# Attention and a leaky-ReLU layer pair on one core: the first two batches by thirds of 192 tokens

## The chip, the core and the metric

The kernel runs on one core of a Trainium2 chip. The metric is device time in microseconds (us) of the whole kernel, the median of several runs. A profile of one execution gives the span (first to last instruction) and what every engine did in it: PE (matmuls; PEld are its weight loads), DVE, ACT and POOL (elementwise work), SP (it issues most DMAs), and the 16 DMA engines.

## The reference

Eight batches, eight heads, 576 tokens, head size 64. Heads 0 to 3 ("plain") see the last 32 tokens; heads 4 to 7 ("dilated") see the last 32 tokens at distance 0, 4, 8, ... The heads' outputs side by side are the rows `x` (4608 x 512) of two weight matrices with a leaky ReLU between them.

```python
mask_plain = (rel >= 0) & (rel < window)                       # window = 32
mask_dil = (rel >= 0) & (rel < window * dilation) & (rel % dilation == 0)   # dilation = 4
scores = np.where(mask, scale * q @ k.T, -1e9)
attn = softmax(scores)
x = (attn @ v), heads side by side
h = x @ w_in                       # 512 -> 2048
out = np.maximum(0.01 * h, h) @ w_out   # 2048 -> 512
```

## The kernel before

**Tiling.** Tokens are taken in fours: token 4n + r is row n, residue r, so that a dilated head of one residue is a plain window over n. Two batches make a pair m; a pair's 1152 rows are three chunks of 384 columns in `xt`: chunk 0 is the first 384 of batch 0, chunk 1 the first 384 of batch 1, chunk 2 the last 192 of both. For every chunk there are 16 "ups" (`up`, four matmuls over the 512 inputs, then a leaky ReLU by ACT into `gt`) and three "downs" of 128 rows (`down`, 16 matmuls, an eviction, stores). From the ninth tile on, four tiles go together through `group`, with fewer products and sums of weights; the last three chunks take `up_fast`.

**Attention of the first two batches** (`b < EARLY`). `load_group` loads q, k and v of one kind of heads: 128 rows of four tokens, that is 512 of the 576 tokens, as 128 partitions x 1 KB per head. POOL, DVE or ACT cast them to fp16 (L272, L270) into `nat`. `turn` lets PE transpose four 128 x 128 blocks each of q and k (L692) and moves them from PSUM into `slots` (L644, L642) in the order that the scores need. `unit` is one set of scores, exponential, mask, values and norm: in `BY_PE` the mask is added by a matmul with the identity (L837), the scores are L854 (or L840), the values L898 (or L892) and the sums L886; ACT forms the reciprocal as exp(-ln), and DVE multiplies into `xt` (L936). A dilated unit covers two residues x 96 rows, or, for the last 48 rows, four residues x 48 ("small"). The last 64 tokens come apart (`load_rest`, `part == 1`): loads of 16 rows per head into `stg[4]` and into every fourth partition of v, a cast into `rest`, 8 transposes for all heads. For batch 0 the plain heads' v is not loaded a second time in its overlapping layout; PE makes it from the rows with shifted identities (`permute`, L347, and L353 for the rest). Later batches are loaded in another layout (128-byte packets to 32 partitions) and turned by DVE and POOL (L674, L679, L685), in `late_unit` and `across`.

**Weights.** `load_w` brings w_in in 8 blocks of 512 KB (n = 0 to 7: row block n % 4, column half n // 4) and w_out in 8; POOL and DVE cast them in halves. An up of columns j needs the four row blocks of its column half.

**Order.** The whole program is a list of tasks with dependencies, a cost and a priority each. `_Plan.run` places them on engines by these costs, and the program issues them in that order. On the chip every engine works its own list in order and waits on semaphores. `FIRST` writes out the order of SP's first loads: b and v are q, k and v of batch 0 by kind of heads, i and o are blocks of w_in and w_out, 0 is the rest of batch 0, c, y and 1 the same of batch 1. `RANKS` gives the priorities of the attention parts. Buffers are rings (`ring`): a new user waits for the last user of its slot. Where the plan leaves PE a gap, filler matmuls on the tile `warm` into a spare bank are put in (L1595); eight stand at the start (L1489).

```python
FIRST = "bvbviiii0iiiicoocoyoooooy1"
...
first_ups = [up(0, j, 0, 384, x_done[0, 0], first_acts) for j in range(N_UPS)]
...
halves = [(0, 192), (192, 192)] if m == 0 and n_c % 3 == 2 else [(0, 384)]
```

Chunk 0's ups start when batch 0's first part has been normed; the other eight of its ups come later in the plan, by the due times `begins` (20.8 us a chunk). PSUM has eight banks: `sps0`, `tp`, two `ops`, two `hps` (ups), two `fps` (downs). During batch 0's first part `fps[1]` also takes k's transposes, and `hps` scores and values.

Of the kernel before, what the change touches and what calls it, by code (L numbers as in the profile page):

```python
# [14 lines left out]
WIN = 32  # L15
AHEAD, LATE = 5.0, 4.0
# [4 lines left out]
FIRST = "bvbviiii0iiiicoocoyoooooy1"  # L21
RANKS = ((10.0, 6.0), (10.0, 0.5), (15.0, 2.0), (25.0, 2.0))


def _constants():

    ident = np.eye(128, dtype=np.float16)
    p = np.arange(128)[:, None]
    key = p - 32
    c = np.arange(96)[None, :]  # L30
    qry = 4 * (c % 24) + c // 24
    rel = qry - key
    band = (rel >= 0) & (rel < WIN)
    first = band & (key >= 0)
    rel0 = c - p
    d0 = (rel0 >= 0) & (rel0 < WIN)
    c1 = np.arange(48)[None, :]
    rel1 = 96 + c1 - (16 + p)
    d1 = (rel1 >= 0) & (rel1 < WIN)
    rel2 = 96 + c1 - np.where((p < 64) & (p % 4 == 0), 128 + p // 4, p)  # L40
    d2 = (rel2 >= 0) & (rel2 < WIN)
    bias = np.where(np.concatenate([first, band, band, d0, d2], axis=1), 0.0, -60000.0)
    parts = [ident, bias, first, band, band, d0, d1, d1, d0, d2]
    return np.concatenate([x.astype(np.float16) for x in parts], axis=1)
# [98 lines left out]
def kernel(  # L143
# [24 lines left out]
    TILED = ((0, 0), (0, 1), (1, 0))  # L168
    BY_PE = ((0, 0), (0, 1), (1, 0))
    POOL_MASK = (1,)  # L170
    BLOCKS = tuple(range(16))
    N_UPS = 8
# [20 lines left out]
    NBIAS, NMASK = 288 + 96 + 48, 288 + 288 + 48  # L193
# [3 lines left out]
    B_PL, B_D0, B_D2 = 128, 128 + 288, 128 + 288 + 96  # L197
# [8 lines left out]
    vst = [v_all[:, 2048 * i:2048 * i + 2048] for i in range(2)]  # L206
    v_two = [v_all[:, 1024 * i:1024 * i + 1024] for i in range(NVS)]
# [37 lines left out]
    tpk = fps[1].bitcast(FP16)  # L245
# [6 lines left out]
    def took(n, size):  # L252
        for a, ta, b, tb in ((4, 9.0, 128, 15.0), (128, 15.0, 256, 19.0), (256, 19.0, 1024, 48.0),
                             (1024, 48.0, 2048, 85.0)):
            if size <= b:
                return n * (ta + (tb - ta) * (size - a) / (b - a)) / 16e3
        return n * size / 25.6 / 16e3

    def load(queue, dst, src, n, size, deps, prio, slow=1.0):
# [3 lines left out]
                        LATE if prio > -1500 + len(FIRST) else 0.8 if prio >= AFTER else 0.0)  # L263
# [35 lines left out]
    def clear_slots(slots, prio, deps):  # L299
        for i in slots:  # L300
            t_zero[i] = ([clear("DVE", qbd[i][64:128, 0:S], 0.34, 0.0, prio, deps),
                          clear("DVE", qbd[i][0:64, S:2 * S], 0.34, 0.0, prio, deps)],
                         [clear("DVE", kt[i][:, 0:PAD], 0.1, 0.0, prio, deps)])

    clear_slots(range(4), -2000, [])
    t_one = clear("POOL", ones, 0.1, 1.0, -1995)
    t_ones = {}
    TWO_ONES = float(np.ones(2, np.float16).view(np.float32)[0])

    def clear_ones(slots, deps, prio=-700):  # L310
        for i in slots:
            t_ones["d", i] = clear("POOL", at(vd[i].bitcast(FP32), 0, 128, D // 2, [64, 16], [1, D // 2]),
                                   0.48, TWO_ONES, prio,
                                   deps)
            t_ones["p", i] = clear("POOL", at(vp[i].bitcast(FP32), 0, 128, D // 2, [64, 12], [1, D // 2]),
                                   0.38, TWO_ONES, prio,
                                   deps)

    clear_ones(range(2), [], -1980)
    t_vr = [clear("POOL", vst[i][0:64, 1024:2048], 1.0, 0.0, -1970 + i) for i in range(2)]  # L320
    SPREAD, SHIFT = 36, 67

    def ident_at(tl, off, step, prio):
        t = clear("DVE", tl.bitcast(FP32), 0.3, 0.0, prio)
        return add("DVE", 0.2, 0.2, [t, t_id], lambda e: nc.vector.tensor_copy(
            out=at(tl, 0, 128, off, [step, 128]), in_=ident), prio)

    t_spread = ident_at(el[0], SPREAD, 4, -1985)
    t_shift = ident_at(el[1], SHIFT, 1, -1600)
    v_half = pair1  # L330
    permuted = []

    def permute(tiles, deps, prio, rest_from=None):

        if rest_from is None:
            n, b_users = tiles[0] // 2, []
            b_old = rings["TPK"][-1] if n else []
            bk = fps[n]
        else:
            n, b_old = ring("F", 2, b_users := [])  # L340
            bk = fps[n]

        def pe(e):
            for y, t in enumerate(tiles):
                for r in range(4):
                    s = 96 * t - 32 - r + SPREAD
# [3 lines left out]
                if t == 5:  # L350
                    for r in range(4):
                        for i in range(2):
                            nc.tensor.matmul(bk[:, 256 * y + 128 * i:256 * y + 128 * i + 128],  # L353
                                             el[1][0:64, 3 - r:131 - r],
                                             at(turned[i], 0, 64, r * D, [256, 2], [1, D]),
                                             start=False, stop=(r == 3), skip_group_check=True)
        t_p = add("PE", 0.11 * (4 * len(tiles) + 4 * (5 in tiles)), 0.25,
                  deps + b_old + [t_spread] + [t_shift] * (5 in tiles), pe, prio)
        permuted.append((t_p, b_users))
        res = []  # L360
        for j in range(2):
            vt = vp[j]

            def fn(e, j=j, vt=vt):
                o = at(vt, 0, 128, tiles[0] * 128, [768, 2], [128, 2], [1, D])
# [5 lines left out]
            t = add((("ACT", 0.3), ("DVE", 0.36)), None, 0.2, [t_p] + kept_old[j], fn, prio)  # L371
            b_users.append(t)
            res.append(t)
        if rest_from is None:
            rings["F"][n].extend(res)
# [4 lines left out]

    kept, v_late, seen_ones = {}, {}, {}
    kept_old = [[], []]

    def stage_slot(early, users):
        if early:
            return ring("STG", NST, users)
        if "STG4" not in rings:
            assert len(rings["STG"]) == 2 * NST
            rings["STG4"] = rings["STG"][-NST:-1]
        return ring("STG4", NST - 1, users)  # L390
# [5 lines left out]
    def load_group(b, g, prio, prio_v):  # L396
# [3 lines left out]
        early = b < EARLY  # L400
        first = b == 0
        base = (b * H + 4 * g) * HS
        stage, loads = [], []
        for o, src in ((0, q), (1, k)):
            sn, s_old = stage_slot(early, s_users := [])
            st = stg[sn]
            if first:
                lo = [load("SP", at(st, 0, 128, j * 512, [256, 2], [1, 256]),
                           dram(src, base + 2 * j * HS, [4 * D, 128], [HS, 2], [1, 256]),
                           256, 1024, s_old, prio + 0.3 * j + 0.1 * o) for j in range(2)]  # L410
            elif early:
                lo = [load("SP", at(st, 0, 128, 0, [256, 4], [1, 256]),
                           dram(src, base, [4 * D, 128], [HS, 4], [1, 256]),
                           512, 1024, s_old, prio)]
            else:
                lo = [load("SP", at(st, 32 * a, 32 * a + 32, 0, [32, 36], [1, 32]),
                           dram(src, base + (a // 2) * 2 * HS + (a % 2) * 32,
                                [D, 32], [32 * D, 36], [1, 32]),
                           1152, 128, s_old, prio) for a in range(4)]
# [3 lines left out]
        lv, v_free = [], []  # L423
        if early:
            vn, v_old = ring("VST", 2, v_users := [])
            vs = vst[vn]
            v_free = [v_users, v_users]
            if dil:
                lv = [[load("SP", at(vs, 0, 128, 0, [256, 4], [1, 256]),
                            dram(v, base, [4 * D, 128], [HS, 4], [1, 256]), 512, 1024, v_old,  # L430
                            prio_v)]] * 2
                v_late[b] = vs, v_old, v_users
            if first and not dil:
                t_l = load("SP", at(vs, 0, 128, 0, [256, 4], [1, 256]),
                           dram(v, base, [4 * D, 128], [HS, 4], [1, 256]), 512, 1024, v_old, prio_v)
                c_h = [cast(v_half[:, 512 * i:512 * i + 512], vs[:, 512 * i:512 * i + 512], 512, [t_l],
                            prio_v, ("POOL", "ACT")) for i in range(2)]
                v_users += c_h
                v_late[b, 0] = vs, v_old, v_users
                v_late["cast"] = c_h  # L440
                made = [{0: [], 1: []}, {0: [], 1: []}]
            for j in range(2 if not dil and not first else 0):
                n = 12
                lj = [load("SP", at(vs, 0, 128, (12 * j + 12 - n) * D, [D, n], [1, D]),
                           dram(v, base + (1152 * j - 32) * D, [D, 128], [96 * D, n],
                                [1, D]), 128 * n, 256, v_old, prio_v + 0.3 * j)]
                lv.append(lj)
            v_from = [(vs, 2 * j * (256 if dil else 384), 256 if dil else 384) for j in range(2)]
        else:
            if "V2" not in rings:  # L450
                rings["V2"] = [sum(rings["VST"][-2:], [])] * NVS
# [206 lines left out]
    def turn(b, hp, part, prio):  # L658
# [89 lines left out]
        else:  # L748
# [39 lines left out]
            if b:  # L788
                ev += q_users
# [863 lines left out]
```

## Time and profile before

| what | value |
|---|---|
| median of 3 runs | 305.9 us (305.5 to 306.68) |
| the profiled execution | 306.29 us |
| its span | 304.5 us |
| PE busy | 294.4 us (97%), 2970 matmuls |
| DVE, ACT, POOL busy | 231.0, 188.7, 132.3 us |
| DMA | 51.09 MB, mean 168 GB/s |
| granted TensorE clock | 1.0 |
| last store done after the last matmul's end | 3.8 us |

The profile also lists the costliest groups of instructions (columns: line, engine, operation, output<-inputs, shapes, count | busy us, mean ns of one | idle before):

```profile
L1091 PE MATMUL hps<-xt,w_in 128*128 128x384 f16 (+1 forms) x640 | 111.7, 310 | 0.8 <-DVE w_in L272 0.6
L1364 PE MATMUL fps<-w_out,gt 128*128 128x256 f16 x416 | 53.6, 273 | 0.0
L272 POOL CAST nat<-stg 128x576 f16<-128x576 f32 (+1 forms) x53 | 43.0, 834 | 9.7 <-DMA stg<-in_q_dram 3.5
```

Matmuls overlap, so the mean of one is longer than the distance from one start to the next; what a matmul takes of PE's time is that distance. The filler counts as busy too.

### The profile page before, as it was taken

Reading aid. Unit: us, or ns where it says so; the run is one execution under the profiler, and the core shown is the slowest. Engines: PE = TensorE matmul, PEld = TensorE weight load, DVE = VectorE, ACT = ScalarE, POOL = GpSimd, SP = SyncE. Lnnn points to the kernel's source line nnn. Section 1 sums busy time; section 2 is a strip of 40 time slices with the busy share of each in tenths; the row PEclk is TensorE's granted clock in tenths of the full one; section 3 lists DMA queues with packets and bytes.
Section 4 is the critical chain, followed back from the end, with each engine's and each line's share of the span. In section 5 each row is a group of like instructions: output and inputs, shape, how many; then the busy total and the mean of one; then the engine's idle time right before and its main releaser. Section 6 shows DMA issues by size and latency. Waiting matters only on the chain.

```text
span 304.5 us, 7869 instructions
## 1 busy us (share of the span) xinstructions
PE 294.4 (97%) x2970; PEld 225.4 (74%) x2970; DVE 231.0 (76%) x478; ACT 188.7 (62%) x458; POOL 132.3 (43%) x179
## 2 busy tenths in 40 slices
PE   6889999999999999997999999999999999999994
PEld 3646655667777676786777777887788999999984
DVE  6875875689686869959888779879775899697552
ACT  3857854795556678464766567456565688767230
POOL 5469555393674949159094668665000000000000
PEclk9999999999999999999999999999999999999999
DMA  7999999999999899976999969793102110031124
GB/s 241 404 370 392 407 289 201 239 201 167 253 171 196 190 188 196 174 180 134 183 161 221 204 136 194 159 208 80 37 2 72 34 37 2 11 91 32 32 76 146
DMA packets 160390, 51.09 MB, mean 168 GB/s; under 512 B 137632, under 2 KB 157024, under 8 KB 160352
## 3 DMA queue, kind: packets, MB, share of 16 engines
q1 hardware_dynamic: 159520, 49.86, 68.3%
q10 hardware_dynamic: 832, 0.73, 0.8%
q8 instruction: 23, 0.38, 0.5%
q14 instruction: 15, 0.12, 0.1%
HBM read 41.13 MB, written 9.44 MB: 166 GB/s over the span
## 4 chain that ended last, share of the span: by engine, by line
PE 90%; DVE 5%; ACT 3%; DMA 1%; issue 1%; DVEq 0%
PE hps L1091 29%; PE fps L1364 26%; PE fps L1275 9%; PE ops L1015 3%; PE hps L1188 3%; PE ops L1188 3%; PE ops L1063 2%; PE sps L1188 2%; PE tp L1188 1%; PE tp L692 1%; PE ops L1364 1%; PE tp L982 1%; PE sps L982 1%; DVE ee L1008 1%; PE fps L347 1%; PE tp L975 1%
## 5 line engine op out<-in xcount | busy, mean ns | idle before, releaser
L1091 PE MATMUL hps<-xt,w_in 128*128 128x384 f16 (+1 forms) x640 | 111.7, 310 | 0.8 <-DVE w_in L272 0.6
L1102 ACT ACTIVATE gt<-hps 128x384 f16<-128x384 f32 (+1 forms) x160 | 72.8, 461 | 43.8 <-PE hps L1091 41.5
L1091 PEld LDWEIGHTS <-w_in 128*128 128x128 f16 x640 | 56.7, 98 | 26.3 <-DVE w_in L272 1.0
L1364 PEld LDWEIGHTS <-gt 128*128 128x128 f16 x672 | 64.4, 98 | 9.7
L679 POOL COPY slots<-turned 64x576 f16<-64x576 f16 x48 | 36.3, 757 | 47.4 <-DVE turned L674 45.5
L1364 PE MATMUL fps<-w_out,gt 128*128 128x256 f16 x416 | 53.6, 273 | 0.0
L272 POOL CAST nat<-stg 128x576 f16<-128x576 f32 (+1 forms) x53 | 43.0, 834 | 9.7 <-DMA stg<-in_q_dram 3.5
L1275 PE MATMUL fps<-w_out,gt 128*128 128x512 f16 x128 | 32.4, 379 | 0.0
L1037 DVE TENSOR_TENSOR rc<-ops,recs 96x384 f16<-96x384 f32 x48 | 25.7, 538 | 0.3
L1393 ACT COPY stg<-fps 128x512 f32<-128x512 f32 (+1 forms) x24 | 12.8, 532 | 14.4 <-PE fps L1364 14.4
L1008 DVE TENSOR_TENSOR ee<-ee,con 128x576 f16<-128x576 f16 x24 | 17.2, 722 | 3.5 <-ACT ee L994 3.5
L1033 DVE RECIPROCAL recs<-ops 96x6 f32<-96x6 f32 x48 | 8.7, 181 | 14.7 <-PE ops L1015 12.5
L1401 DVE TENSOR_TENSOR osb<-fps,stg 128x512 f32<-128x512 f32 x18 | 12.4, 687 | 9.7 <-PE fps L1364 5.6
L272 POOL CAST vd<-v_all 128x1024 f16<-128x1024 f32 (+2 forms) x20 | 18.0, 918 | 2.7 <-DMA v_all<-in_v_dram 2.7
L1211 ACT ACTIVATE gt<-stg 128x384 f16<-128x384 f32 x36 | 18.0, 524 | 1.1 <-DVE stg L1205 1.1
L1275 PEld LDWEIGHTS <-gt 128*128 128x128 f16 x128 | 11.6, 98 | 9.1
L644 DVE COPY slots<-tp 64x128 f16<-64x128 f16 (+7 forms) x42 | 13.4, 333 | 6.3 <-PE tp L692 5.6
L674 DVE STREAM_TRANSPOSE turned<-nat 128x576 f16<-128x576 f16 x24 | 17.7, 751 | 0.0
L685 DVE STREAM_TRANSPOSE slots<-nat 128x576 f16<-128x576 f16 x24 | 17.7, 745 | 0.0
L1008 DVE TENSOR_TENSOR el<-el,con 128x576 f16<-128x576 f16 x24 | 15.0, 630 | 2.7 <-ACT el L994 2.5
L1188 PEld LDWEIGHTS <-w_in 128*128 128x128 f16 x192 | 16.4, 98 | 0.5 <-DVE w_in L1119 0.3
L994 ACT ACTIVATE ee<-sps 128x288 f16<-128x288 f32 x24 | 9.8, 409 | 8.4 <-PE sps L982 5.8
(158 smaller groups left out, 529.3 us busy)
## 6 DMA issues: line engine op xcount, KB each, us to landing
stg<-in_q_dram SPq DMA_DIRECT2D x48, 144.0 KB, 3.2
stg<-in_k_dram SPq DMA_DIRECT2D x48, 144.0 KB, 2.9
v_all<-in_v_dram SPq DMA_DIRECT2D x24, 256.0 KB, 3.8
v_all<-in_v_dram SPq DMA_DIRECT2D x24, 192.0 KB, 3.2
gt<-in_moe_w_in_dram SPq DMA_DIRECT2D x5, 512.0 KB, 7.1
out_dram<-osb SPq DMA_DIRECT2D x22, 96.0 KB, 2.0
out_dram<-osb SPq DMA_DIRECT2D x40, 48.0 KB, 1.8
out_dram<-osb SPq DMA_DIRECT2D x25, 64.0 KB, 2.2
```

The lines of the kernel that those rows point to most:

```text
L272: ENG[e].tensor_copy(out=dst, in_=src)
L674: lambda e: nc.vector.transpose(xb, na[:, 0:S]), prio)
L679: lambda e, p0=p0, hh=hh: nc.gpsimd.tensor_copy(out=at(qb, p0, p0 + 64, hh * S + o, *od), in_=at(xb, p0, p0 + 64, i, *id_)), prio, 0.0, "m ...
L685: lambda e: nc.vector.transpose(kb[:, PAD:PAD + S], na[:, S:2 * S]), prio)
L1008: nc.vector.tensor_tensor(out=x, in0=x, in1=mk, op=ALU.mult)
L1037: nc.vector.tensor_tensor(out=at(xb, 0, 96, 768 * n + 64 * i, [256, 3], [128, 2], [1, D]), in0=at(ot, 0, 96, 0, [130, 3], [65, 2], [1, D]) ...
L1091: nc.tensor.matmul(ht[:, 0:n], at(w_in, 0, 128, i * DFF + j // 2 * 256 + j % 2, [2, 128]), at(xt[m % 2], 0, 128, i * 1152 + x0, *dims), st ...
L1102: lambda e: nc.scalar.activation(out=gt[c % NG][:, j * n_c + x:j * n_c + x + n], in_=ht[:, 0:n], func=AF.Prelu, alpha=0.01),
L1188: nc.tensor.matmul(cell[:, n * z:n * z + n], lhs(2 * p + z, i), rhs(i), start=first and z == 0 and i == 0, stop=z == 1 and i == 1, skip_gr ...
L1211: lambda e: nc.scalar.activation(out=at(g, 0, 128, j * n_c + n * y, [n_c, 2], [1, n]), in_=at(src, 0, 128, 0, [n, 2], [1, n]), func=AF.Pre ...
L1275: nc.tensor.matmul(ft, g[:, j * n_c + tt * 128:j * n_c + tt * 128 + 128], w_out[:, j * DM:j * DM + DM], start=(j == 0), stop=(j == NJ - 1))
L1364: nc.tensor.matmul(bk[:, x:x + HN], tl[:, off + j * step:off + j * step + 128], rhs(j), start=first and x == 0 and j == 0, stop=j == HJ - ...
```

## The change

The first two batches are no longer taken as 512 tokens and a rest of 64 but as three thirds of 192 tokens (48 rows of four). `load_third` loads, for each kind of heads, q to partitions 0 to 47 and k to 48 to 95 of one tile, with four heads x 1 KB per partition, and v to 48 partitions (64 to 111 or 16 to 63 in turn). One cast takes q and k of two heads together on 96 partitions, one set of transposes turns both (96 x 128 blocks, `turn_third`), and each move serves two heads. All dilated units are now of the small form (48 rows x 4 residues), with k of the current and the last third side by side in `kt`. `permute` makes v of batch 0 by third; in batch 1 the plain v is loaded in its layout, two loads a third.

Chunk 0's ups are cut in two halves of 192 columns (the first third, the second third) by `up_half`: pairs of j share a bank and one leaky ReLU. Chunk 2's ups stay in halves; the first of them depends on batch 0 alone and is now placed with batch 0 (`UPS`). Masks by PE are now in five of the six thirds (`BY_PE`), twenty units as before. `FIRST` and `RANKS` are written anew (A, a to F, f are the thirds and their v), as are some constants of the planner (`LATE`, `took`). `load_rest`, the shifted identity in `el[1]`, and `part` are gone.

```diff
-AHEAD, LATE = 5.0, 4.0
+AHEAD, LATE = 5.0, 2.5
-FIRST = "bvbviiii0iiiicoocoyoooooy1"
-RANKS = ((10.0, 6.0), (10.0, 0.5), (15.0, 2.0), (25.0, 2.0))
+FIRST = "AaiiBbiiiiiiCcooooDdooooEeFf"
+RANKS = ((-30.0, 5.0), (-8.0, 0.1), (-6.0, 0.1), (-4.0, 0.1), (-3.0, 0.1), (20.0, 2.0))
...
-    TILED = ((0, 0), (0, 1), (1, 0))
-    BY_PE = ((0, 0), (0, 1), (1, 0))
+    BY_PE = ((0, 0), (0, 1), (0, 2), (1, 0), (1, 1))
...
+    def load_third(b, t, prio, prio_v):
+        for g in (1, 0):
+            dil = g == 1
+            base = (b * H + 4 * g) * HS + 192 * t * D
+            sn, s_old = ring("STG", NST - 1, s_users := [])
+            st = stg[sn]
+            lo = [load("SP", at(st, 48 * o, 48 * o + 48, 0, [256, 4], [1, 256]),
+                       dram(src, base, [4 * D, 48], [HS, 4], [1, 256]),
+                       192, 1024, s_old, prio + 0.4 * (1 - g) + 0.1 * o)
+                  for o, src in ((0, q), (1, k))]
...
+            c_qk = [cast(at(na, 0, 96, 512 * j, [D, 2], [128, 4], [1, D]),
+                         at(st, 0, 96, 512 * j, [256, 2], [D, 4], [1, D]), 512, lo + n_old,
+                         prio + 0.4 * (1 - g), ("DVE", "ACT", "POOL") if b == 0 else CENG) for j in range(2)]
...
+        even = t % 2 == 0
+        d0, p0 = (64, 16) if even else (16, 64)
+        ld = load("SP", at(vs, d0, d0 + 48, 0, [256, 4], [1, 256]),
+                  dram(v, base, [4 * D, 48], [HS, 4], [1, 256]), 192, 1024, v_old, prio_v)
...
+    def turn_third(b, t, g, prio):
+            def pe(e, j=j):
+                for r in range(4):
+                    nc.tensor.transpose(bk[:, 384 * j + 96 * r:384 * j + 96 * r + 96],
+                                        na[0:96, 512 * j + 128 * r:512 * j + 128 * r + 128],
+                                        ident[0:96, 0:96])
...
+    def up_half(c, y, p, done, acc):
+        x0, x_in, x_out = ((48 * y, [[96, 4], [1, 48]], [[48, 4], [1, 48]]) if c == 0 else
+                           (384 + S * y, [[1, 192]], [[1, 192]]))
+        def part_of(i):
+            def fn(e):
+                for z in range(2):
+                    nc.tensor.matmul(ht[:, 192 * z:192 * z + 192],
+                                     at(w_in, 0, 128, i * DFF + p * 256 + z, [2, 128]),
+                                     at(xt[0], 0, 128, i * 1152 + x0, *x_in),
...
+    UP_AT = {0: (0.0, 5.2), 2: (12.0, 45.0)}
+    UPS = (((0, 0, 0),), ((0, 0, 4), (0, 1, 0), (0, 1, 4)), ((2, 0, 0), (2, 0, 4)))
...
+                    if b == 0:
+                        for c, y, p in [(c, y, p) for c, y, p0 in UPS[t] for p in range(p0, p0 + 4)]:
+                            acts = all_acts.setdefault(c, [[] for _ in range(NJ)])
+                            up_half(c, y, p, x_done[c, y], acts)
```

## The prediction

> **What bounds the kernel now.** I first read busy time by stretches of 5 us (columns: the stretch, then the busy time of PE, its weight loads, DVE, ACT and POOL with instructions, the granted clock, the DMA share, GB/s).
>
> ```profile
> 0.00:5.00 5.00, 3.71 (x10) 1.28 (x10) 3.42 (x17) 1.33 (x2) 3.85 (x12) 1.00 0.56 180
> 15.00:20.00 5.00, 4.71 (x47) 2.53 (x44) 4.48 (x12) 3.37 (x11) 2.50 (x5) 1.00 1.05 356
> 20.00:25.00 5.00, 4.16 (x30) 2.35 (x29) 2.98 (x11) 2.34 (x5) 5.00 (x9) 1.00 1.03 386
> 25.00:30.00 5.00, 5.00 (x53) 3.36 (x52) 2.92 (x7) 3.64 (x9) 5.00 (x12) 1.00 1.06 403
> 35.00:40.00 5.00, 5.00 (x43) 3.19 (x41) 3.25 (x9) 2.78 (x7) 2.99 (x6) 1.00 1.03 420
> ```
>
> From 25 us PE has no idle time and its clock is full; until 40 us the DMA share is 1.0 too. So PE is busy to the end once it has work, and what can be won is the time before. PE's timeline shows where that begins (start, duration, instruction, idle before):
>
> ```profile
> 18.00 1.25 PE L1595 MATMUL fps<-warm 128*128 128x512 f16 x5
> 19.09 1.16 PE L1091 MATMUL hps<-xt,w_in 128*128 128x384 f16 x6
> 20.89 0.50 PE L1091 MATMUL hps<-xt,w_in 128*128 128x384 f16 x2 [0.64 <-DVE w_in L272]
> 21.22 0.38 PE L1595 MATMUL fps<-warm 128*128 128x512 f16 x1
> 21.80 1.46 PE L1091 MATMUL hps<-xt,w_in 128*128 128x384 f16 x8 [0.20 <-ACT gt L1102]
> ...
> 103.04 0.68 PE L1063 MATMUL ops<-con,rc 96*128 96x96 f16 x12
> ...
> 142.55 0.36 PE L1015 MATMUL ops<-vp,ee 128*128 128x65 f16 x6 [1.60 <-DVE ee L1008]
> ```
>
> L1595 on "warm" is filler, useful to nobody; the last is at 21.22. From 21.80 to the last matmul PE waits only twice, 0.17 us at 121.8 and 1.60 us at 142.5; then 3.8 us of eviction and store. Work done by 21.8, priced by distance between starts: 8 times 4 transposes at 0.23 = 1.84; 8 units with scores at 0.33 and values at 0.30 = 5.04; 16 spreading matmuls (L347) at 0.11 = 1.76; 8 up-projections at 0.1625 = 1.30. Sum 9.9, so **11.9 us are lost** at the start.
>
> What keeps PE waiting is data. POOL's timeline shows the weight blocks landing, and the one-microsecond stretches the rates:
>
> ```profile
> 13.48 0.61 POOL L272 CAST w_in<-gt 128x512 f16<-128x512 f32 x1 [0.65 <-DMA gt<-in_moe_w_in_dram]
> 14.76 0.61 POOL L272 CAST w_in<-gt 128x512 f16<-128x512 f32 x1 [0.66 <-DMA gt<-in_moe_w_in_dram]
> 16.04 0.61 POOL L272 CAST w_in<-wst 128x512 f16<-128x512 f32 x1 [0.67 <-DMA wst<-in_moe_w_in_dram]
> ...
> 8.00:9.00 1.00, 0.61 (x7) 0.21 (x4) 0.64 (x2) 0.98 (x3) 0.93 (x2) 1.00 1.07 377
> 13.00:14.00 1.00, 0.76 (x8) 0.50 (x6) 0.97 (x3) 1.00 (x3) 0.52 (x1) 1.00 1.05 430
> 17.00:18.00 1.00, 0.71 (x8) 0.29 (x6) 0.73 (x3) 1.00 (x5) 0.12 (x1) 1.00 1.12 290
> ...
> 46.00:50.00 4.00, 4.00 (x34) 2.19 (x33) 2.06 (x6) 1.92 (x6) 2.90 (x5) 1.00 1.21 192
> ```
>
> Blocks of 512 KB come every 1.28 us (about 415 GB/s); q, k and v, in packets of 1 KB, move at about 376 (377 at 8 us). The dip at 17 us is where the small loads of the last 64 tokens run (`load_rest`), which the change drops. Block 0's cast starts 0.9 us after its last byte by the summed rates; I use 0.9 as landing delay.
>
> **The change, part by part.**
>
> *PE work.* Transposes: 80 at 57.5 ns (0.23/4) become 96 over 96 partitions; row 103.04 is that form, 12 in 0.51 us to the next start, 42.5 ns: 4.60 to 4.08, -0.52. Spreading: 1.76 at 13.46 us plus 0.97 and 0.55 at 26.48 (3.28) becomes 24 at 0.11 (2.64): -0.64. Eight dilated units have 8 value matmuls of 48 columns (0.14) for 4 of 96 (0.11): +0.24. Chunk 0's up-projection is 128 of 192 columns (0.0825, from 0.66 for 8) for 64 of 384 (0.1625): +0.16. Scores cost the same (4 x 0.041 against 2 x 0.0825), masks by PE stay 20, chunk 2 was in halves already. Sum **-0.76 us**, all of it on PE's path.
>
> *When data arrives.* SP's new order is third A of batch 0 (q and k of the dilated heads, then of the plain ones, then two v loads; six loads, 1.18 MB), two w_in blocks, third B, six w_in, C, w_out blocks, D and so on. SP issues a load in 0.51 us, 0.197 MB each, 386 GB/s, so issue doesn't bound. By before's summed bytes for the first 6 us, then 376 and 415: A complete at 6.25 (with constants), two blocks 8.8, B 11.9, six blocks 19.5, C's first pair 20.55. With 0.9 landing: B's second q,k pair 11.7, w_in block 3 15.3, block 7 20.4, C's first pair 21.4, D's 30.1, E's 39.65. DVE's clears end near 5.0, as before (4.92): two of `kt` grow from 0.1 to about the 0.30 of a 64x288 one, one clear of `el` and one copy (0.5 together) go. POOL clears three v tiles (0.92 each), five 512-word tiles (0.47) and two of 384 (0.40), 6.0 us with `ones` against 3.7, so it is free at 6.7; its first cast waits for v at 7.0 anyway. 0 on the path; if v came at once, 0.5.
>
> *PE's walk*, in its own order:
> 1. The second group of B is transposed after landing (11.7), POOL cast 0.6 and 0.34: done 12.7. Useful by then: 16 transposes 0.68, four units 2.58, spreading 0.88, 16 transposes 0.68: 4.8. Lost 7.9.
> 2. B's scores wait for ACT and DVE to move q and k (0.58 and 0.42, one behind the other): +0.7. Then scores 0.66, spreading 0.88, values 0.66, scores 0.66, first up parts 0.16 reach 16.4; block 3 is cast at 15.75. Lost 8.6.
> 3. Four pairs of up-projections with values between (4.0 us) end at 20.45; the fifth needs block 7, cast by 21.0: +0.55. These parts hold PE's queue, so what could run (the second half's first pairs, which share the two hps banks in turn) waits too.
> 4. C's transposes stand next, ready at 21.4 + 0.6 = 22.0 against 21.3: +0.7. Lost **9.85**.
> After that PE reaches D's transposes at 30.75 (ready 30.7) and E's at 40.1 (ready 40.25): level, with nothing to spare.
>
> Gain at the start 11.9 - 9.85 = **2.05 us**. Waits 2 to 4 (1.95) are bounded by nothing from below; the 1.77 us of later waits may vanish or come again elsewhere, since DVE's order changes; I keep them.
>
> *Moves at no cost.* Chunk 2's first half goes from about 71 us to the thirties; it is work either way. DVE, ACT and POOL have about the same instructions (casts 0.42 to 0.61 each as now) and after 25 us PE covers them. The planner's constants change order alone.
>
> *The unknown: loads to 48 partitions.* No row has 1 KB packets to 48 partitions. Best, they move like 128-partition loads, 376 GB/s: 3.14 us a third. Worst row: at 46 us the q and k loads, each to 32 partitions (128-byte packets), move 192 GB/s at DMA share 1.21: 6.15 us, x = 3.0 more per third. I take 376: the packet is the same 1 KB, and q beside k covers 96 partitions within one group. Since PE runs level with arrivals, x counts 2.33 times at C, 3.33 at D, 4.33 at E.
>
> [...]
>
> **Sum.** 304.5 - 2.05 - 0.76 = 301.7 us of span. The profiled execution took 306.29, 1.79 around its span; the median is 305.9, so 305.9 - 2.8 = **303.1**.
>
> **Rivals.**
> - *Narrow loads are slow* (the other side). Place: SP's loads A to E; price 4.33x; the gain of 2.8 is gone at x = 0.65 us (311 GB/s), and at x = 1.0 (285 GB/s) it is slower by 1.5. At 192 GB/s: 303.1 + 13.0 = 316.1. For: the dip to 290 under small loads, 192 under 32-partition ones, PE level with arrivals. Against: those have short packets or few rows. 0.40, of which 0.07 falls within 0.5% of before.
> - *The gain is given back later*: PE reaches batches 2 and 3 2.8 us sooner, while DMA is near full to 130 us, and waits there: 305.9. Against: 99.34 starts chunk 3 though its batch was done by 92.5. 0.07.
> - *Better than forecast*: waits 2 to 4 and the two later ones vanish: 303.1 - 1.95 - 1.77 = 299.4. 0.11.
> - The forecast: 0.42.
>
> About 0.5% (1.5 us) is what a measurement can tell from none. Faster 0.42 + 0.11 = 0.53; same 0.07 + 0.07 = 0.14; slower 0.33. The likeliest case alone spans 301 to 304.4. The range goes from 299.3 down at the good end to x = 1.5 (303.1 + 6.5 = 309.6); beyond lie about 0.05 and 0.15.
>
> **What would show it.** Right: the first complete up-projection near 16.4, no filler after about 13 us, casts of w_in block 7 near 20.4 to 21, C's transposes at 22, later idle under 2 us. Wrong: GB/s clearly under 376 during A and B, D's transposes after 31 with PE idle before them (slow loads); PE idle between 80 and 140 us (given back); w_in cast late with data there (POOL or DVE behind).

## The result, and the profile after

| | before | after |
|---|---|---|
| median (lowest to highest), 6 runs each | 305.86 us (305.5 to 306.68) | 321.88 us (319.29 to 324.1) |
| ratio, 95% interval | | 1.0499 (1.0441 to 1.0557) |
| profiled execution; its span | 306.29; 304.5 | 319.63; 317.8 |
| first 62 us: PE busy; mean granted clock | 57.55; 1.00 | 50.18; 0.89 |

The change makes the kernel 5% slower. The profiled execution is 2.25 us under the median, so the trace shows a little less than the whole loss. Medians are of all runs, ratios of the fast ones (one of after's six, 324.1, was slow). From the page of after (span; busy time of PE; the granted clock in 40 slices; the shares of the chain that ended last):

```profile
span 317.8 us, 8130 instructions
...
PE 301.3 (95%) x3083; PEld 232.6 (73%) x3083; DVE 226.1 (71%) x464; ACT 192.1 (60%) x453; POOL 138.6 (44%) x189
...
PEclk9798799799999999999999999999999999999999
...
PE 79%; DMA 17%; DVE 2%; SPq 0%; POOL 0%; issue 0%; POOLq 0%
```

DMA has gone from 1% of the chain to 17%, and the clock is no longer full in the first 60 us. PE's timeline of after shows where PE stands still (last bracket: idle before, and what ended it):

```profile
22.32 1.00 PE L974 MATMUL hps<-xt,w_in 128*128 128x192 f16 x10 [1.23 <-POOL w_in L273]
...
29.57 0.82 PE L974 MATMUL hps<-xt,w_in 128*128 128x192 f16 x4 [2.34 <-POOL w_in L273]
30.84 0.82 PE L642 MATMUL tp<-con,nat 96*128 96x96 f16 x8 [0.45 <-DVE nat L273]
31.46 1.80 PE L974 MATMUL hps<-xt,w_in 128*128 128x192 f16 x10
...
55.81 0.82 PE L642 MATMUL tp<-con,nat 96*128 96x96 f16 x8 [2.29 <-DVE nat L273]
```

The first complete up-projection comes at 22.3 us (forecast 16.4), C's transposes at 30.84 (22.0), D's at 43.53 (30.75), E's at 55.81 (40.1). At 31.46 ten matmuls of 192 columns take 1.6 us to the next start, 0.16 each; at full clock they take 0.0825 (0.66 us for 8 in before). Between the two profiled executions PE's last matmul ends 13.5 us later: 8.4 us of it are longer distances from one matmul's start to the next, most of that at the halved clock, and 5.1 us are more idle time and filler. The 1 us stretches of after (the third number from the end is the granted clock, then DMA share, GB/s):

```profile
7.00:8.00 1.00, 0.36 (x9) 0.37 (x10) 0.69 (x2) 0.74 (x2) 0.07 (x1) 1.00 1.27 209
18.00:19.00 1.00, 0.73 (x7) 0.66 (x7) 1.00 (x4) 0.50 (x2) 0.94 (x3) 1.00 1.02 406
26.00:27.00 1.00, 0.80 (x11) 0.61 (x8) 0.29 (x1) 0.31 (x1) 0.89 (x2) 1.00 1.14 202
31.00:32.00 1.00, 1.00 (x12) 0.97 (x11) 0.00 (x1) 1.00 (x3) 0.00 (x0) 0.50 1.03 338
```

At 7 and 26 us the DMA engines are as busy as ever (share over 1) and move about 205 GB/s: loads of thirds. At 18 us w_in blocks go by at 406. The chain of waits of after between 7 and 55 us consists of loads; each piece starts 0.02 us after the one above has landed, because SP issued its load only then (they are the 12th, 20th, 28th, 36th and 44th load on SP):

```profile
7.08 8.14 DMA stg<-in_k_dram
...
15.24 13.60 DMA xt<-in_moe_w_in_dram
...
28.86 6.11 DMA con<-consts
...
34.98 9.95 DMA v_all<-in_v_dram
...
44.95 10.29 DMA stg<-in_k_dram
```

The second is w_in block 7: 13.6 us from issue to landing (its like took 6.2 to 10.1 in before), although it is not one of the narrow loads; POOL casts it at 28.89, forecast 20.4 to 21.0:

```profile
28.89 1.18 POOL L273 CAST w_in<-xt 128x512 f16<-128x512 f32 x2 [2.00 <-DMA xt<-in_moe_w_in_dram]
```

So there are four suspects: the rate of the narrow loads, the halved clock, an order planned for loads that come too early, and SP's limit on loads under way.

### The profile page after: what moved, and what is told of

Same layout as the page of the kernel before. It is cut to its first block, busy times and chain, and to the rows that moved or that the text cites. A ratio compares the mean times of both kernels' runs of the same rounds, so it can differ in the third digit from the quotient of the medians.

```text
span 317.8 us, 8130 instructions
## 1 busy us (share of the span) xinstructions
PE 301.3 (95%) x3083; PEld 232.6 (73%) x3083; DVE 226.1 (71%) x464; ACT 192.1 (60%) x453; POOL 138.6 (44%) x189
## 4 chain that ended last, share of the span: by engine, by line
PE 79%; DMA 17%; DVE 2%; SPq 0%; POOL 0%; issue 0%; POOLq 0%
PE fps L1252 25%; PE hps L948 22%; PE fps L1161 8%; DMA stg<-in_k_dram 7%; DMA xt<-in_moe_w_in_dram 4%; PE ops L873 3%; DMA v_all<-in_v_dram 3%; PE hps L1074 3%; PE ops L1074 3%; PE hps L974 3%; PE ops L921 2%; DMA con<-consts 2%; PE sps L1074 2%; PE tp L1074 1%; PE ops L1252 1%; PE sps L840 1%
## 5 line engine op out<-in xcount | busy, mean ns | idle before, releaser
L948 PE MATMUL hps<-xt,w_in 128*128 128x384 f16 x448 | 86.1, 326 | 0.0
L955 ACT ACTIVATE gt<-hps 128x384 f16<-128x384 f32 x112 | 54.8, 492 | 30.8 <-PE hps L948 29.2
L948 PEld LDWEIGHTS <-w_in 128*128 128x128 f16 x448 | 40.4, 98 | 20.4 <-issue 0.2
L273 POOL CAST nat<-stg 128x576 f16<-128x576 f32 (+1 forms) x57 | 44.8, 808 | 23.2 <-DMA stg<-in_k_dram 14.3
L543 POOL COPY slots<-turned 64x576 f16<-64x576 f16 x48 | 39.0, 813 | 17.4 <-DVE turned L538 15.7
L974 PE MATMUL hps<-xt,w_in 128*128 128x192 f16 x256 | 28.9, 264 | 3.8 <-POOL w_in L273 3.8
L974 PEld LDWEIGHTS <-w_in 128*128 128x128 f16 x256 | 22.7, 105 | 5.7 <-POOL w_in L273 4.4
L985 ACT ACTIVATE gt<-hps 128x384 f16<-128x384 f32 x32 | 15.6, 491 | 11.2 <-PE hps L974 10.7
L1289 DVE TENSOR_TENSOR osb<-fps,stg 128x512 f32<-128x512 f32 x18 | 12.4, 688 | 9.6 <-PE fps L1252 6.4
L273 POOL CAST vp<-v_all 128x768 f16<-128x768 f32 (+1 forms) x18 | 13.0, 733 | 11.7 <-DMA v_all<-in_v_dram 10.5
L866 DVE TENSOR_TENSOR el<-el,con 128x576 f16<-128x576 f16 x24 | 13.6, 568 | 6.0 <-ACT el L852 6.0
```

The lines of the kernel that those rows point to most:

```text
L273: ENG[e].tensor_copy(out=dst, in_=src)
L543: lambda e, p0=p0, hh=hh: nc.gpsimd.tensor_copy(out=at(qb, p0, p0 + 64, hh * S + o, *od), in_=at(xb, p0, p0 + 64, i, *id_)), prio, 0.0, "m ...
L948: nc.tensor.matmul(ht[:, 0:n], at(w_in, 0, 128, i * DFF + j // 2 * 256 + j % 2, [2, 128]), at(xt[m % 2], 0, 128, i * 1152 + x0, *dims), st ...
L955: lambda e: nc.scalar.activation(out=gt[c % NG][:, j * n_c + x:j * n_c + x + n], in_=ht[:, 0:n], func=AF.Prelu, alpha=0.01),
L974: nc.tensor.matmul(ht[:, 192 * z:192 * z + 192], at(w_in, 0, 128, i * DFF + p * 256 + z, [2, 128]), at(xt[0], 0, 128, i * 1152 + x0, *x_in ...
```

## Experiments

**Loads by themselves.** A kernel that only loads, in sets that differ in the partitions they go to.

```diff
+    def some(i, p0, n=48, step=1, heads=4):
+        nc.sync.dma_start(at(bufs[i], p0 * row, [step * row, n], [256, heads], [1, 256]),
+                          dram(src, (i // 3 * 8 + 4 * (i % 2)) * HS, [4 * D, n], [HS, heads], [1, 256]))
```

> The kernel only loads, in twelve sets of six loads each, with a pause after every set, and stores zeros: nothing of the reference is computed. Nine sets move 384 KB per load in packets of 1 KB and differ only in the partitions they go to; one goes to partitions 0-31 with 256 KB a load, one is 128 partitions by 4 KB as the weight blocks are. Theory 1 (the rate follows which partitions a load reaches): 128 partitions about 376 GB/s; 0-47, 48-95 and 64-111 alone and 0-47 in turn with 48-95 about 200 to 230; 0-47 in turn with 64-111 hardly more, if loads in one queue do not share; every second of 96 partitions clearly above 280; 96 partitions about 300. Theory 2 (rate follows the packets, and what is slow in the changed kernel comes from other traffic or from the limit on open loads): all sets of 1 KB packets within 10% of 376 GB/s.

That first one failed as a measurement: between sets I cleared whole tiles, 1.76 us each, and each load waited for its tile, so loads of 384 KB, one per 2.14 us, could not pass 184 GB/s on average. Only the DMA share told something: it was 0.58 for 128 partitions at 195 GB/s (6 to 14 us) and 1.08 for 0-47 at 152 (22 to 30 us). Without the pacing:

> As the first load kernel, but with nothing that paces the loads: twelve at once per set, 192 KB each to 48 partitions (256 KB to 64 or 128, 384 KB to 96, 512 KB in the set of 4 KB packets), a short pause between sets. Nothing of the reference is computed. Order: 128 partitions; 0-47; 48-95; 64-111; 16-63; 32-79; 0-47 and 48-95 in turn; 0-47 and 64-111 in turn; even and odd of 96 in turn; the changed kernel's third twice (0-47, 48-95, twice, then 64-111 and 16-63); the same with q and k even and odd; 0-63; 0-63 and 64-127 in turn; 96 partitions; 128 partitions by 4 KB. [...] If it is only the number of partitions in a load that counts, all sets of 48 partitions give the same rate.

From the stretches of that kernel (one execution), each inside one set, with the sets' order as in the expectation (last: GB/s): 0-47; 48-95; 64-111; 0-47 and 64-111 in turn; even and odd in turn; the changed kernel's third; 128 partitions by 4 KB.

```profile
24.00:32.00 8.00, 0.99 (x7) 0.00 (x0) 1.00 1.15 154
40.00:44.00 4.00, 0.92 (x6) 0.00 (x0) 1.00 1.11 273
52.00:62.00 10.00, 1.08 (x7) 0.00 (x0) 1.00 1.10 144
...
108.00:115.00 7.00, 1.23 (x8) 0.00 (x0) 1.00 1.14 214
120.00:127.00 7.00, 1.23 (x8) 0.00 (x0) 1.00 0.94 267
133.00:141.00 8.00, 1.11 (x8) 0.00 (x0) 1.00 1.14 196
...
222.00:231.00 9.00, 1.07 (x7) 0.00 (x0) 1.00 1.03 415
```

The others: 16-63 151, 32-79 277, 0-47 and 48-95 in turn 227, a third with q and k even and odd 235, 0-63 200, the two halves in turn 237, 96 partitions 226. (The first set, 128 partitions by 1 KB, was still paced by the opening clears.) It is not the number of partitions alone that counts: 48 partitions move 144 or 277 GB/s by where they lie. The changed kernel's third, 1.18 MB at 196 GB/s, takes 6.0 us where I had put 3.14.

**The kernel before with narrow loads.** No thirds and no half up-projections; only q and k of batches 0 and 1 go to halves of the partitions, or to every second one (the diff shows the halves; the other starts at `h * row` and steps by `2 * row`). The casts of the first batch wait for both pieces.

```diff
-                lo = [load("SP", at(st, 0, 128, 0, [256, 4], [1, 256]),
-                           dram(src, base, [4 * D, 128], [HS, 4], [1, 256]),
-                           512, 1024, s_old, prio)]
+                lo = [load("SP", piece(st, j), from_dram(src, base, j),
+                           256, 1024, s_old, prio) for j in range(2)]
...
+        return bass.AP(tensor=tl.tensor, offset=tl.offset + 64 * h * row,
+                       ap=[[row, 64], [256, 4], [1, 256]])
```

> The kernel before with one thing different: q and k of the first two batches, 4.2 MB, go in the same number of bytes and 1 KB packets to partitions 0-63 and 64-127 in turn (256 KB each), in place of 128 partitions at once; for the first batch that is the same number of loads as before. No thirds, no halves. If the partitions of a load set its rate (about 200 GB/s for half of them), its early loads take up to 9 us more and the kernel 309 to 315 us, with 1 us stretches near 200 GB/s where it had 376. If not, 305 to 307 us.

> The control of the kernel in halves: the same number of loads, bytes and 1 KB packets, 64 partitions each, but the even and the odd partitions in turn in place of 0-63 and 64-127. If it matters which partitions a load reaches, the early stretches are back near 350 to 376 GB/s and the time near 306 to 308 us (the casts of the first batch still wait for both loads). If it matters only that a load has 64 partitions, the stretches stay at 210 to 245 GB/s and the time at 315 to 318 us.

Halves: 316.84 us, ratio 1.0353 (1.0314 to 1.0392), 11 us slower. Even and odd: 309.07, 1.0096 (1.0068 to 1.0125). Both are 1 to 2 us over what I expected. Same stretch in both, first halves:

```profile
10.00:11.00 1.00, 0.89 (x7) 0.70 (x7) 0.62 (x2) 0.06 (x1) 0.97 (x2) 0.50 1.11 211
```

and even and odd:

```profile
10.00:11.00 1.00, 1.00 (x9) 0.82 (x8) 0.42 (x1) 0.24 (x1) 0.94 (x2) 0.50 1.10 374
```

Loads, bytes, packets and order are equal; which partitions a load reaches makes 7.8 us. Even and odd do not bring all of the early rate back: over the first 12 us the mean is 208 GB/s for halves, 248 for even and odd and 297 before. Whether that or the casts that now wait for two loads makes the 3 us over before is not separated. The clock is 0.5 in this stretch of both (0.94 and 0.97 over the first 62 us), so it is not what tells their rates apart.

**q and k spread in the changed kernel.**

```diff
-            lo = [load("SP", at(st, 48 * o, 48 * o + 48, 0, [256, 4], [1, 256]),
+            lo = [load("SP", bass.AP(tensor=st.tensor, offset=st.offset + o * st.ap[0][0],
+                                     ap=[[2 * st.ap[0][0], 48], [256, 4], [1, 256]]),
...
-                       at(bk, 0, 128, 48, [384, 2], *id_), 384, tp + old + z[1] + busy, prio, eng))
+                       at(bk, 0, 128, 1, [384, 2], *id_), 384, tp + old + z[1] + busy, prio, eng))
```

> The changed kernel with one thing different: q goes to the even and k to the odd of the 96 partitions, and what reads the transposes takes every second column. Same loads, bytes, packets and order. If the partitions that a load reaches set its rate, q and k of a third (0.79 MB) take about 2.5 us in place of 3.7 us (215 to 320 GB/s), 1.2 us in each of five thirds: 314 to 318 us, with the transposes of the third third near 28 us in place of 30.84. If the order in thirds, the limit on open loads, or the halved up-projections cost the time: within 1 us of 321.9.

322.62 us, ratio 1.0552 (1.0486 to 1.0618): no gain, a miss, and what was expected if the partitions did not matter. The rate of B's loads rose only from 224 to 241 GB/s (11 to 17 us in both) and that of C's from 223 (24 to 30 us in after) to 239 (26 to 32 us here); the two v loads of a third stay on 64-111 and 16-63 (144 and 151 GB/s alone). The start is slower, too: SP takes 3.83 us to issue A's six loads (2.81 in after), the DMA share falls to 0.63 and 0.48 in the stretches at 7 and 8 us (1.27 and 0.83 in after), and B's first transposes come at 17.15 (14.64), while C's are about level (31.17 and 30.84). How much each of the two takes from the gain is not separated.

**The clock.**

```diff
+    FILL = {("T", 0, 0, 0, 0): 5, ("T", 0, 1, 0, 0): 1, (3, 0): 5, (7, 0): 10, ("T", 0, 2, 1, 0): 2,
+            ("T", 1, 0, 1, 0): 12, ("T", 1, 1, 1, 0): 10}
...
+            for _ in range(FILL.pop(key, 0)):
+                w = _Task((("PE", 0.0),), 0.0, [], idle(512, sps0), 0, 0.0, 0, "w")
```

> The changed kernel with 45 filler matmuls of 512 columns (about 0.215 us each, on the bank of sps0) put in front of the seven places where PE stood idle: 5 before the second transposes, 1 and 2 before the next thirds, 5 and 10 before the up-projections that wait for w_in blocks 3 and 7, 12 and 10 before the transposes of the first two thirds of batch 1. Nothing else moves. If the halved clock after idle stretches is what makes the difference to the forecast, the clock stays at 1.0 and the time falls by 5 us or more, to 317 or less. If the loads set the pace and the clock's loss lies beside them, the clock still stays at 1.0 but the waits before the last two thirds grow by what is saved: 320 to 322.5 us, the transposes of batch 1 at 43.5 and 55.8 us as now.

322.96 us, ratio 1.0519 (1.045 to 1.0588), clock 1.000 in the profiled execution. PE's timeline of that kernel before D's and E's transposes:

```profile
39.27 2.75 PE L1488 MATMUL sps<-warm 128*128 128x512 f16 x12
41.86 0.51 PE L644 MATMUL tp<-con,nat 96*128 96x96 f16 x8
...
51.89 2.32 PE L1488 MATMUL sps<-warm 128*128 128x512 f16 x10 [0.34 <-ACT ee L724]
54.04 0.51 PE L644 MATMUL tp<-con,nat 96*128 96x96 f16 x8
```

The transposes come 1.7 us sooner than in after, with every filler done, yet the whole is no faster: this execution waits 1.17 us at 156 us and 2.6 us between 172 and 181 us for later loads and what follows them. Against before, idle time and filler are 10.0 us more and the distances between matmul starts 3.1 us longer, 13.1 together where after has 13.5: what the clock gives back goes into filler. The time is that of the expectation's second case within the noise; its place for the transposes is not. And this is no clean price of the clock. The cast that D's transposes wait for starts at 40.49 (43.05 in after) and E's at 51.26 (55.33), so the data itself comes 2.6 and 4.1 us sooner here, and the fillers hold PE 0.9 and 2.3 us beyond it. A full clock got in this way gains nothing; what it would be worth without that hold stays open.

**The plan.** The planner is told how slow the loads are; the loads stay, or q and k are spread as well.

```diff
-                       192, 1024, s_old, prio + 0.4 * (1 - g) + 0.1 * o)
+                       192, 1024, s_old, prio + 0.4 * (1 - g) + 0.1 * o, 1.55)
...
-                  dram(v, base, [4 * D, 48], [HS, 4], [1, 256]), 192, 1024, v_old, prio_v)
+                  dram(v, base, [4 * D, 48], [HS, 4], [1, 256]), 192, 1024, v_old, prio_v, 2.25)
```

> The changed kernel with only the planner told of slower narrow loads (its time for q and k times 1.55, for v times 2.25, near what the load kernel measured), so that it orders PE, DVE, ACT and POOL for them and puts fillers where PE will wait. Loads are the same. If a good part of the loss is an order that was planned for loads that come too early (up-projections that hold PE's queue while others could run): 314 to 318 us. If the loads set the pace whatever the order: 319.5 to 323 us, with a clock of 1.0.

> q and k on even and odd partitions, and the planner told of it (1.35 for q and k, 2.25 for v). By the load kernel a third takes 5.4 us in place of 6.0, so by x alone 2 to 3 us under the changed kernel; 314 to 320 us if order and rate add, 320 to 323 if neither is worth anything by itself. Still slower than before in any case, since 96 or 48 partitions were never over 275 GB/s.

321.08 us, ratio 1.0497 (1.0452 to 1.0542), and 318.93, 1.0431 (1.0364 to 1.0498). The order alone is worth nothing that can be told from noise; with the spread loads perhaps 3 us, but its interval overlaps after's. Neither comes near before.

**Wide loads.** The changed kernel with its order untouched, but each load of a third to 128 partitions, with fewer or with more bytes than the 192 KB it moves.

```diff
-            lo = [load("SP", at(st, 48 * o, 48 * o + 48, 0, [256, 4], [1, 256]),
-                       dram(src, base, [4 * D, 48], [HS, 4], [1, 256]),
+            lo = [load("SP", at(st, 0, 128, 256 * o, [256, 1], [1, 256]),
+                       dram(src, base, [4 * D, 128], [HS, 1], [1, 256]),
```

> The changed kernel, its order, casts, transposes, half up-projections untouched, but each q, k and v load of a third goes to 128 partitions with 128 packets of 1 KB (128 KB in place of 192 KB), and the casts read them (part of the data twice), so the values are not the reference's. At one issue per 0.51 us six loads take about 3.1 us, which is the 3.14 us a third that the forecast used. If the rate of the narrow loads is the term that failed and the rest of the forecast's walk holds: 301 to 306 us, the third third's transposes near 22 to 24 us and batch 1's last near 40 to 43. If the thirds or the halved up-projections cost time by themselves: 310 us or more.

> The same with 256 packets of 1 KB to 128 partitions per load (256 KB, a third more bytes than the changed kernel moves); the values are not the reference's either. A third is 1.57 MB, about 4.2 us at 376 GB/s, 1.05 us more than the forecast's: by its own terms 303.1 + 4.33 x 1.05 = 307.6; 305 to 311 us, far under 321.9 although more bytes are moved. If bytes and not partitions set the pace: over 322 us.

306.38 us with 128 KB, ratio 1.0000 (0.9973 to 1.0027), and 311.6 with 256 KB, 1.0144 (1.0098 to 1.019). Even with a third more bytes the kernel is 10.3 us faster than after; with a third fewer it is 15.5. The 192 KB of a narrow load lie between the two, so by interpolation the thirds and the halved up-projections cost at most a few us by themselves: the narrow loads cost 10 to 15 of the 16 us, together with the halved clock that follows the waits for them (with 128 KB the clock is 1.00 over the first 62 us, 0.89 in after). But 306.4 is not 303.1 either: w_in block 7 is cast 3 us late in it.

**How many loads.** The loads of SP, with two of ACT's at the start, go through eight semaphores in turn, and the ninth waits until the first has landed (the 12th, 20th and later loads of the chain above start 0.02 us after that); in after's list of instructions (numbers count SP's loads):

```
6 L263 DMACopy gt_88<-in_moe_w_in_dram 128x1024 [waits DMAHW0_49]
...
13 L263 DMACopy v_all<-in_v_dram 48x4x256 [waits DMAHW7_49]
14 L263 DMACopy wst_93<-in_moe_w_in_dram 128x1024 [waits DMAHW0_49]
```

The two kernels below move the bytes of the 128 KB kernel in half as many loads (the diff is that of the second).

```diff
-            lo = [load("SP", at(st, 0, 128, 256 * o, [256, 1], [1, 256]),
-                       dram(src, base, [4 * D, 128], [HS, 1], [1, 256]),
+            lo = [load("SP", at(st, 0, 128, 0, [256, 2], [1, 256]),
+                       dram(src, base, [4 * D, 128], [HS, 2], [1, 256]),
...
+            lo[1].fn = lambda e: None
```

> The kernel with 128 KB loads, whose third takes six loads, with the same bytes in half as many: per third one load of 256 KB each for q, k and v (for batch 1 v's plain part stays as it was), which both head groups' casts read; values not the reference's. It differs too in that three clears of v are shorter. In the kernel with 128 KB loads w_in blocks came about 3 us later than forecast, and its ninth load could be issued only when the first had landed, eight being open at a time. If that limit is what delays the blocks: the four first blocks and the third third come 2 to 3 us sooner, and the time is 302 to 304.5 us against 306.4. If it is not: 306 to 307.5 us.

314.31 us, ratio 1.0266 (1.0232 to 1.03): a miss, and no answer. The early part did come sooner (block 7 cast at 22.07), but the planner had put the later work in another order, and PE waited 6.2 us between 157 and 193 us. So once more with the order kept:

> The kernel with 128 KB loads once more, now with the order of every engine kept as it is there (the last kernel's planner had rearranged all that follows): of each pair of loads (q and k of a head group; for batch 0 the two of v) the first moves 256 KB and the second is left out, so that a third takes three issues instead of six for the same bytes; the values are not the reference's. If the limit of eight open loads delays the w_in blocks and the third third: block 7 cast near 22 us (24.0 there), the third third's transposes near 23.5 (25.0), and 304 to 305.5 us against 306.4. If the early loads are no longer what sets the end once they are wide: 306 to 307 us although the blocks come sooner.

305.34 us (305.08 to 305.68, 11 runs), ratio 0.9974 (0.9965 to 0.9984). POOL's timeline has the cast of block 7, first with six loads a third:

```profile
24.00 1.36 POOL L273 CAST w_in<-xt 128x512 f16<-128x512 f32 x2
```

then with three:

```profile
20.24 1.17 POOL L273 CAST w_in<-xt 128x512 f16<-128x512 f32 x2
```

From 14 to 20 us the one moves 290 GB/s at a DMA share of 0.95, the other 402 at 1.03. So half as many loads bring block 7 3.8 us sooner; C's transposes come at 24.45 in place of 25.01. That this is the limit is not shown, and the traces speak for the issuing itself: before it issues block 7 SP waits 2.4 us for landings with six loads a third and 3.1 us with three, so those waits are not what grew, but six more loads stand ahead of block 7 and single issues take over 1 us. SP's timeline has the issue of block 7 with six loads a third (start, duration):

```profile
12.96 1.48 SPq L263 DMA_DIRECT2D xt<-in_moe_w_in_dram  x1
```

and with three:

```profile
10.39 0.33 SPq L263 DMA_DIRECT2D xt<-in_moe_w_in_dram  x1
```

At the end about 1 us of it is left; by the two ratios it is 0.8 us, give or take 0.9, hardly clear of the noise. None of these kernels beats before with a right result, and the runs point to none: a load of a third as it is laid out, 48 rows with four heads side by side, reaches 48 partitions and not 128.

## Why the prediction was wrong

- *The unknown: loads to 48 partitions.* This is the step that failed. I took 376 GB/s because "the packet is the same 1 KB, and q beside k covers 96 partitions within one group". Measured: 196 GB/s for a whole third, x = 2.9 us in place of 0, well past the break-even of 0.65. q beside k does not help: 0-47 alone moves 154, 0-47 and 48-95 in turn 227, even one load to 96 partitions 226. Nor do two halves in turn come near 376: 0-47 and 64-111 move 154 and 144 alone and 214 in turn, 0-63 alone 200 and 0-63 with 64-127 in turn 237. The worse bound, 192 GB/s from the 32-partition loads, was nearly the right value; that its row, with 128-byte packets, comes so close may be chance. "Against: those have short packets or few rows" was no argument, and that rows of 1 KB were my nearest row was the wrong likeness: partitions, not packets, were what the change altered. With the loads widened to 128 partitions the time falls to 306.4 (fewer bytes) and 311.6 (more).
- *Rival "narrow loads are slow"* was the right case with too low a price: 316.1 at 192 GB/s against 321.9. Of the 5.8 us missing, 3.3 are missing with wide 128 KB loads as well (306.4 against 303.1): about 1 goes with the number of loads, the rest is in the next points. The other 2.5 are not separated; the halved clock or SP's longer waits when each load lasts longer (block 7's 13.6 us) would do it, but no run shows either alone.
- *"SP issues a load in 0.51 us, 0.197 MB each, 386 GB/s, so issue doesn't bound"* left two things out: in the first 62 us of after SP waits 33 us in all for landings before it may issue, and with wide loads six issues a third in place of three still delay block 7 by 3.8 us. With three loads a third, block 7's cast at 20.24 is what the summed bytes forecast (20.4).
- *PE work, -0.76.* Mis-sized. Summing PE's timeline by distances between starts, less listed idle and fillers, gives 287.4 us for before and 288.6 for the kernel with three wide loads, +1.1, so this term was 1.9 us too good. The 96-row transposes take 47.5 ns each where row 103.04 gave 42.5, the up-projections of 192 columns 88 for 82.5, the mask matmuls 184 for 165; short waits under the listed ones are in these.
- *PE's walk.* As to what waits for what it was right for after: block 3, block 7, then C's transposes, and then waits before D's and E's, so that slow thirds add up. In its times it was too short: in the kernel with three wide loads, where block 7 is cast as forecast, C's transposes come at 24.45 (22.0), D's at 34.1 (30.75), E's at 43.7 (40.1), and PE is no longer level with arrivals but behind them. There idle time and filler in the first 62 us are 0.8 us under before, not 2.05; the waits after that, which the forecast kept, are 0.8 us shorter. With the 1.9 of the PE work that is 2.3 us, about what lies between 305.3 and 303.1.
- *"Its clock is full"* did not hold in after, where PE idles: 0.5 for some 13.6 of the first 61 us. The drops come with the waits for the narrow loads, since the clock is full with the 128 KB wide ones (1.00 over the first 62 us). The fillers brought no gain with a full clock, but they do not show that the clock costs nothing of its own.
- *Given back later.* Not in after's profiled execution, but the executions with fillers and with spread loads waited 3.8 and 4.5 us between 150 and 185 us for later loads and the work behind them, against 0.2 in after. It is there for a kernel whose loads are late and whose PE is not.

## What to carry to other kernels

Cutting work into smaller pieces can also cut the partitions of its loads, as here: before pricing such a change, ask which partitions each load reaches, not how long its packets are, and let a row with few partitions outweigh a row with the same packet (here 48 partitions moved 144 to 277 GB/s with packets of 1 KB). Where a load had to be narrow, every second partition moved faster than one half (374 against 211 GB/s in the same stretch above, 267 against 227 for 48 of 96 partitions in the load kernel); in the changed kernel, where the v loads stayed as they were and SP issued A's loads later, q and k spread so gained nothing (322.62 us against 321.88). When an unknown has ends far apart and the walk is level with arrivals, the worse end times the number of pieces is the forecast to beat.

## What was not expected of the hardware

- Equal loads of 48 rows of 1 KB move from 144 (64-111) to 277 GB/s (32-79) by where they lie, and 96 partitions in one load (226) less than 48 well placed ones.
- After PE stood still for 2.3 us (27.2 to 29.57) the granted clock was 0.5 from 29.4 to 36.3 us, and after 2.3 us at 53.5 from 56.75 to 60.2; a wait of 1.23 us at 21 us was not followed by a drop, one of 1.13 us at 6.5 us was, from 9.0 to 12.4. So the three drops last 6.8, 3.4 and 3.4 us. How long a wait it takes stays open.
- A 512 KB load to 128 partitions (block 7) took 13.6 us among narrow ones, with five other blocks and two narrow loads open when it was issued, where its like took 6.2 to 10.1 in before.
